# Mask, sums of exponentials and new memory in the tiling of the projections, and tile 0's projections in small pieces

## The chip, the cores and the metric

The kernel runs on one core of a Trainium2 chip. The metric is the device time of one execution in microseconds (us). The engines named below are TensorE (PE; its weight loads are listed apart as PEld), VectorE (DVE), ScalarE (ACT), GpSimd (POOL) and the queues that issue DMAs (SPq).

## What is computed

A block of text (2048 tokens of 512 numbers) goes through two branches, mixed by a gate for each token. Branch B is an MLP over all tokens at once. Branch A is attention with a recurrent memory: the tokens are cut into 64 segments of 32, and each segment's output for its eight memory rows is the next segment's memory, so the segments are one serial chain.

```python
def _A_ref(x, mem0, Wq, Wk, Wv, Wo, seg_len):      # H = 32 heads of 128, M = 8, seg_len = 32
    mask = (idx[:, None] < M) | (idx[:, None] >= idx[None, :])
    mem = mem0
    for s in range(n_seg):                          # 64 segments
        xs = x[:, s * seg_len:(s + 1) * seg_len, :].copy()
        h = jnp.concatenate([mem, xs], axis=1)      # 8 + 32 rows
        q = jnp.einsum('btd,dhe->bhte', h, Wq)      # k and v likewise
        ...
        scores = jnp.where(mask[None, None], scores, -1000000000.0)
        p = _softmax(scores, axis=-1)
        o = jnp.einsum('bhqk,bhke->bhqe', p, v)
        o = jnp.einsum('bhte,hed->btd', o, Wo)
        mem = o[:, :M, :].copy()                    # the next segment's memory
        outs.append(o[:, M:, :])

def _B_ref(x, w1, b1, w2, b2):
    y = _layernorm(x, axis=-1)
    h = _gelu(jnp.einsum('bsd,df->bsf', y, w1) + b1)
    return jnp.einsum('bsf,fd->bsd', h, w2) + b2

return g * a + (1 - g) * b                          # g = sigmoid((x * gate_w).sum(-1))
```

## The kernel before

The MLP comes first; then the loop over segments. Four segments make a tile of 128 tokens. A segment's first 24 tokens ride with its memory rows as 32 columns (`hT`); the last 8 tokens of each of the four segments are projected together ahead of time, as "side work" for the next tile (`left_v`, `left_qk`). Nearly all matmuls of the loop use a quarter of TensorE's array: 128 rows by 32 columns (`tile_position=(0, 32 * j)`), four side by side, written 128*32 in the profile. Attention over V uses 32 rows by 128 columns (32*128). The mask, the sums and the new memory use the whole array (128*128).

```python
def qk_unit(bk, G, t, h0, h1, kc):                                   # L211; v_unit is L222
    n = (h1 - h0) * 32
    for j in range(4):
        nc.tensor.matmul(bk[32 * j:32 * j + 32, 0:n], lhsT=G[:, kc, :], rhs=W5[t][:, kc, h0:h1, j, :],
                         start=(kc == 0), stop=(kc == KC - 1), tile_position=(0, 32 * j))

def left_qk(T, t, hf):                 # side work; left_v is built alike
    h0, h1 = HF[hf]
    bk = side([P, 512])
    side_k = side_n[0]
    for kc in range(KC):
        qk_unit(bk, GLs[T], t, h0, h1, kc)
        if kc < KC - 1:
            yield                      # a piece of four matmuls ends here
    def ev():
        ...                            # transpose and copies, queued for VectorE
    later(dve_q, ev, side_k)
    yield

def mask_mm():
    B = bank(7, [P, 512])
    S = B[:, 0:NG * EW].rearrange("p (i e) -> p i e", e=EW)
    nc.tensor.matmul(S, lhsT=ident[:], rhs=MkA[:].unsqueeze(2).to_broadcast([P, 4, 2, EW]),   # L360
                     start=True, stop=True, skip_group_check=True)
    return B, S
```

The projections of tile 0 have no segment to run beside, so they run beside the last three blocks of the MLP. Each `yield` of `setup` hands back to the MLP's loop over units (`up`: four matmuls, `down`: two).

```python
def setup():
    ...
    for vb in range(2):
        for _ in left_v(0, vb):        # all 16 matmuls at once
            pass
        flush(act_q)
        yield
    for hf in range(2):
        for t in range(2):
            for _ in left_qk(0, t, hf):
                pass
            flush(dve_q)
            yield
    left_v_in(0)
...
for u in range(NBLK * FC):             # 88 units of the MLP
    ...
    if blk >= NBLK - 3 and u % 4 == 0:
        next(pre, None)
```

A segment of the loop, cut:

```python
for bi, (t, h0, h1) in enumerate(BANKS):                     # projections of Q and K, L211
    ...
scores(S, s, 0, 3 * NG // 4)                                 # scores and V (L222) mixed
...
nc.scalar.activation(out=E[:, :, 0:16], in_=S[:, :, 0:16], func=ACTF.Exp, scale=scale, accum_out=hist[:, s, 0:1])     # L670
nc.scalar.activation(out=E[:, :, 16:EW], in_=S[:, :, 16:EW], func=ACTF.Exp, scale=scale, accum_out=hist[:, s, 1:2])
sm = bank(nc_, [P, NG, 8])
nc.tensor.matmul(sm[:], lhsT=BO[:], rhs=E[:, :, 8:16], start=True, stop=False)       # L673, first sums
nc.tensor.matmul(sm[:], lhsT=BO[:], rhs=E[:, :, 0:8], start=False, stop=True)        # L674
...
run_fill(5 + (si == 3))                                      # side work
nc.vector.reciprocal(out=R[:, 0:8 * NG]..., in_=sm[:])       # L677
nc.vector.tensor_tensor(out=Pm[:]..., ...)                   # L679
av(Um, 8, s, V, Pm, 8, 0, 0)                                 # attention of the memory rows, L384, L389
sr = B[:, 0:NG * 32].rearrange("p (i q) -> p i q", q=32)     # the mask's bank
nc.tensor.matmul(sr, lhsT=BO[:], rhs=E[:, :, 16:48], start=True, stop=False, skip_group_check=True)                   # L684, second sums
nc.tensor.matmul(sr[:, :, 24:32], lhsT=BO[:], rhs=E[:, :, 48:56], start=False, stop=True, skip_group_check=True)      # L685
...                                                          # Um to UTT, L688
nc.vector.reciprocal(out=R[:, 8 * NG:]..., in_=sr)           # L689
run_fill(1)                                                  # side work
for half in range(2):                                        # output projection, L233, and wsb, L708
    ...
S_next = mask_mm()                                           # the next segment's mask, L360
av_x(s - 1, (ne, na, nc_, nb))                               # attention of x of the segment before
run_fill(2 * (si == 3))                                      # side work, fourth segment of a tile only
for m in range(KC):                                          # new memory, L719
    nc.tensor.matmul(aT[:, m, :], lhsT=wsb[:, m * P:(m + 1) * P], rhs=Sel[:, 0:M], start=False, stop=True, skip_group_check=True)
nc.vector.tensor_copy(out=hn[:, :, 0:M], in_=aT)             # hT, L720
for _ in fill:                                               # the rest of the side work
    pass
```

Of the kernel before, what the change touches and what calls it, by code (L numbers as in the profile page):

```python
# [23 lines left out]
def kernel(ctx, tc, A_x, A_mem0, A_Wq, A_Wk, A_Wv, A_Wo, A_seg_len, B_x, B_w1, B_b1, B_w2, B_b2, gate_w, out):  # L24
    nc = tc.nc
    P = 128
    _, S, Dm = A_x.shape
    H, Dh = A_Wq.shape[1], A_Wq.shape[2]
    M = A_mem0.shape[1]
# [4 lines left out]
    KC = Dm // P  # L34
# [5 lines left out]
    EW = 16 + 40  # L40
# [212 lines left out]
    def left_qk(T, t, hf):  # L253
# [8 lines that stand above are left out]
            Tv = qk_tr(bk, h0, h1)  # L262
            if t == 0:
                nc.gpsimd.tensor_copy(out=QL[T % 2][:, h0:h1, :], in_=Tv)
            else:
                for hh in range(h0 // 8, h1 // 8):
                    r0 = 8 * hh - h0
                    nc.gpsimd.tensor_copy(out=KL[T % 2][:, :, :, hh, :], in_=Tv[:, r0:r0 + 8, :].rearrange("p g (s c) -> p g s c", c=LEFT))
        later(dve_q, ev, side_k)
        yield  # L270
# [81 lines left out]
    def prep_q(s):  # L352
        T, si = divmod(s, SPT)
        nc.gpsimd.tensor_copy(out=QT[:, :, 32:40], in_=QL[T % 2][:, :, LEFT * si:LEFT * si + LEFT])

    def mask_mm():

        B = bank(7, [P, 512])
        S = B[:, 0:NG * EW].rearrange("p (i e) -> p i e", e=EW)
        nc.tensor.matmul(S, lhsT=ident[:], rhs=MkA[:].unsqueeze(2).to_broadcast([P, 4, 2, EW]),  # L360
                         start=True, stop=True, skip_group_check=True)
        return B, S

    def scores(S, s, i0, i1):
# [119 lines left out]
    def setup():  # L484

        m0p = side([P, KC, M], BF16)
        for kc in range(KC):
            nc.tensor.transpose(m0p[:, kc, :], m0[:, kc * P:(kc + 1) * P], ident[:M, :M])
        nc.vector.tensor_copy(out=hT[0][:, :, 0:M], in_=m0p[:])
        x_left(0)  # L490
        x_left(1)
        prep_h(0)
        yield
        for vb in range(2):
            for _ in left_v(0, vb):
                pass
            flush(act_q)
            yield
        for hf in range(2):
            for t in range(2):  # L500
                for _ in left_qk(0, t, hf):
                    pass
                flush(dve_q)
                yield
        left_v_in(0)
# [21 lines left out]
    for u in range(NBLK * FC):  # L527
        blk, fc = divmod(u, FC)
        T1 = (blk + 1) * TB
        pend.append((u, up(u)))  # L530
        if fc == 2:
            c_act()
        if len(pend) > LAG:
            down(*pend.pop(0))
        if T1 < NT:
            if fc == 1 or fc == 3:
                ys[fc // 2] = norm(T1 + fc // 2)
            elif fc == 5 or fc == 7:
                norm_tr(T1 + fc // 2 - 2, ys[fc // 2 - 2])
        if blk % 2 == 0:  # L540
            if fc in (2, 5, 6, 7) and T1 + 2 < NT:
                bn(T1 + 2 + (2, 5, 6, 7).index(fc) )
            if fc == 8 and T1 + 2 < NT:
                newton(T1 + 2, T1 + 6)

        elif fc in (2, 4, 6, 8):
            T = T1 + (fc - 2) // 2
            if T < NT:
                gates(T, T + 1)
        elif fc == 10 and T1 < NT:  # L550
            gates2(T1, T1 + 4)
        if blk == 0 and fc in (9, 10):
            gates(fc - 9, fc - 8)
        if blk == 1 and fc == 0:
            gates2(0, 2)
        if blk == 1 and fc in (1, 3):
            gates(2 + fc // 2, 3 + fc // 2)
        if blk == 1 and fc == 9:
            gates2(2, 4)
        if blk == NBLK - 2 and fc == 8:  # L560
            ld_wo(H // 2, H)

        if blk >= NBLK - 3 and u % 4 == 0:
            next(pre, None)
    for a in pend:
        down(*a)
# [54 lines left out]
    for s in range(nseg + 2):  # L621
# [11 lines left out]
        if live:  # L633
            B, S = S_next
            na, nb, nc_, nd, ne = ring
            ring = (nd, ne, na, nc_, nb)
            qk_banks = (na, nb, nc_, nd, ne)
            if s >= 2:
                ux_out(s - 2)
                flush(act_q)  # L640
            if s + 1 < nseg:
                prep_h(s + 1)
            if s >= 1:
                prep_q(s)
                x_mul(s - 1)
            flush(dve_q)
            BANKS = [(0,) + HF[0], (1,) + HF[0], (0,) + HF[1], (1, H // 2, 3 * H // 4), (1, 3 * H // 4, H)]
            for bi, (t, h0, h1) in enumerate(BANKS):
                bk = bank(qk_banks[bi], [P, 512])
                for kc in range(KC):  # L650
                    qk_unit(bk, hc, t, h0, h1, kc)
                Tv = qk_tr(bk, h0, h1)
                dst = QT[:, h0:h1, 0:32] if t == 0 else KT[:, h0:h1, :]
                (nc.gpsimd.tensor_copy if bi == 2 else nc.scalar.copy)(out=dst, in_=Tv)  # L654
            V = cw.tile([P, NG, Dh], BF16, tag="V", name="V")
            Vs[s] = V
            vb0, vb1 = bank(na, [P, 512]), bank(nb, [P, 512])
            for kc in range(KC):
                v_unit(vb0, hc, 0, kc)
            nc.scalar.copy(out=v_out(V, 0), in_=vb0[:])  # L660
            flush(dve_q, 9)
            scores(S, s, 0, 3 * NG // 4)
            v_unit(vb1, hc, 1, 0)
            scores(S, s, 3 * NG // 4, NG)
            for kc in range(1, KC):
                v_unit(vb1, hc, 1, kc)
            E = cw.tile([P, NG, EW], BF16, tag="E", name="E")
            R = cw.tile([P, NG * 40], FP32, tag="R", name="R")
            Es[s], Rs[s] = E, R
            nc.scalar.activation(out=E[:, :, 0:16], in_=S[:, :, 0:16], func=ACTF.Exp, scale=scale, accum_out=hist[:, s, 0:1])  # L670
            nc.scalar.activation(out=E[:, :, 16:EW], in_=S[:, :, 16:EW], func=ACTF.Exp, scale=scale, accum_out=hist[:, s, 1:2])
            sm = bank(nc_, [P, NG, 8])
            nc.tensor.matmul(sm[:], lhsT=BO[:], rhs=E[:, :, 8:16], start=True, stop=False)  # L673
            nc.tensor.matmul(sm[:], lhsT=BO[:], rhs=E[:, :, 0:8], start=False, stop=True)  # L674
            nc.scalar.copy(out=v_out(V, 1), in_=vb1[:])
            run_fill(5 + (si == 3))
            nc.vector.reciprocal(out=R[:, 0:8 * NG].rearrange("p (i q) -> p i q", q=8), in_=sm[:])  # L677
            Pm = cw.tile([P, NG, 16], BF16, tag="Pm", bufs=1, name="Pm")
            nc.vector.tensor_tensor(out=Pm[:].rearrange("p i (a q) -> p i a q", q=8), in0=E[:, :, 0:16].rearrange("p i (a q) -> p i a q", q=8),  # L679
                                    in1=R[:, 0:8 * NG].rearrange("p (i q) -> p i q", q=8).unsqueeze(2).to_broadcast([P, NG, 2, 8]), op=ALU.mult)  # L680
            Um = [bank(k, [P, NG, 8]) for k in (nd, ne, na, nc_)]
            av(Um, 8, s, V, Pm, 8, 0, 0)
            sr = B[:, 0:NG * 32].rearrange("p (i q) -> p i q", q=32)
            nc.tensor.matmul(sr, lhsT=BO[:], rhs=E[:, :, 16:48], start=True, stop=False, skip_group_check=True)  # L684
            nc.tensor.matmul(sr[:, :, 24:32], lhsT=BO[:], rhs=E[:, :, 48:56], start=False, stop=True, skip_group_check=True)  # L685
            Tp, sp = divmod(s - 2, SPT)
            for j in range(4):
                (nc.scalar.copy if j % 2 else nc.vector.tensor_copy)(out=UTT[Tp % 2][:, :, j, 24 - 8 * sp:24 - 8 * sp + M], in_=Um[j][:])  # L688
            nc.vector.reciprocal(out=R[:, 8 * NG:].rearrange("p (i q) -> p i q", q=32), in_=sr)  # L689
            run_fill(1)  # L690
        else:
            if s == nseg:
                ux_out(s - 2)
                x_mul(s - 1)
                av_x(s - 1, (ne, na, nc_, 7))
            else:
                ux_out(s - 2)
            flush(dve_q)
            Tp, sp = divmod(s - 2, SPT)
# [15 lines left out]
        run_fill(2 * (si == 3))  # L715
        if s + 1 < nseg:
            aT = S_next[0][:, NG * EW:NG * EW + KC * M].rearrange("p (k m) -> p k m", m=M)
            for m in range(KC):
                nc.tensor.matmul(aT[:, m, :], lhsT=wsb[:, m * P:(m + 1) * P], rhs=Sel[:, 0:M], start=False, stop=True, skip_group_check=True)  # L719
            nc.vector.tensor_copy(out=hn[:, :, 0:M], in_=aT)  # L720
        for _ in fill:
            pass
# [142 lines left out]
```

## Time and profile before

| what | value |
|---|---|
| time, median of 3 runs | 834.87 us (834.65 to 835.76) |
| span of the profiled execution | 832.9 us |
| mean granted clock of TensorE | 0.998 |
| TensorE matmuls | 22405, busy 804.7 us |
| MLP's last three blocks with the projections of tile 0 | about 62 to 99.5 us of the span |
| loop over segments | from about 100 us on |
| an ordinary segment | 10.9 to 11.0 us, the fourth of a tile 11.7 us |

A line of the profile in order of time gives the start and the length in us, the engine, the line of the kernel, the operation, what is written and read, the shape, and how many instructions are merged; in brackets stands how long the engine was idle before, and whose work ended that. The shape 128*32 of a matmul is rows by columns of the array; 128x512 behind it is what streams through. Lengths of matmuls include their way through the array, so matmuls that follow one another closely overlap in the list; starts are the better measure. A share of busy time counts an engine as busy also while a matmul passes through.

### The profile page before, as it was taken

Reading aid. Unit: us, or ns where it says so; the run is one execution under the profiler, and the core shown is the slowest. Engines: PE = TensorE matmul, PEld = TensorE weight load, DVE = VectorE, ACT = ScalarE, POOL = GpSimd, SP = SyncE. Lnnn points to the kernel's source line nnn. Section 1 sums busy time; section 2 is a strip of 40 time slices with the busy share of each in tenths; the row PEclk is TensorE's granted clock in tenths of the full one; section 3 lists DMA queues with packets and bytes.
Section 4 is the critical chain, followed back from the end, with each engine's and each line's share of the span. In section 5 each row is a group of like instructions: output and inputs, shape, how many; then the busy total and the mean of one; then the engine's idle time right before and its main releaser. Section 6 shows DMA issues by size and latency. Waiting matters only on the chain.

```text
span 832.9 us, 49239 instructions
## 1 busy us (share of the span) xinstructions
PE 804.7 (97%) x22405; PEld 495.4 (59%) x22417; DVE 501.7 (60%) x1019; ACT 434.0 (52%) x1245; POOL 273.7 (33%) x625
## 2 busy tenths in 40 slices
PE   6999999999999999999999999999999999999886
PEld 4665555665666665566566556656656656665554
DVE  5764256565666566666656565656656665666553
ACT  3555544555455555555554555455555555555552
POOL 8000234242424333332424242434243243424220
PEclk9999999999999999999999999999999999999999
DMA  9791210100000010101010100000010101010000
GB/s 318 253 391 44 87 32 7 28 12 24 15 23 23 17 28 10 37 11 35 10 27 13 35 11 22 23 20 26 12 34 10 36 10 35 5 35 5 10 5 24
DMA packets 38216, 37.64 MB, mean 45 GB/s; under 512 B 13545, under 2 KB 36434, under 8 KB 36466
## 3 DMA queue, kind: packets, MB, share of 16 engines
q1 hardware_dynamic: 37874, 34.31, 12.4%
q8 instruction: 177, 2.90, 1.5%
q14 instruction: 37, 0.30, 0.1%
q0 software_dynamic: 128, 0.13, 0.1%
HBM read 26.03 MB, written 6.29 MB: 39 GB/s over the span
## 4 chain that ended last, share of the span: by engine, by line
PE 93%; DVE 3%; DMA 1%; issue 1%; SPq 1%; ACT 1%; DVEq 0%; ACTq 0%
PE b L211 35%; PE b L233 18%; PE b L222 17%; PE b L384 5%; PE hp L456 4%; PE bp L473 4%; PE b L360 2%; PE b L369 2%; PE b L684 2%; PE b L719 1%; PE b L389 1%; PE b L673 1%; DMA Wo_sb<-in_A_x_dram 1%; PE b L320 1%; PE b L373 0%
## 5 line engine op out<-in xcount | busy, mean ns | idle before, releaser
L217 DVE STREAM_TRANSPOSE Tt<-b 128x512 f32<-128x512 f32 (+1 forms) x384 | 225.6, 613 | 85.5 <-PE b L211 71.8
L211 PEld LDWEIGHTS <-hT 128*32 128x32 bf16 x5120 | 134.7, 97 | 100.0 <-DVE hT L720 15.4
L233 PE MATMUL b<-Wo_sb,UTT 128*32 128x256 bf16 (+1 forms) x4736 | 162.7, 285 | 1.2 <-ACT UTT L619 0.8
L222 PE MATMUL b<-Wv_sb,hT 128*32 128x512 bf16 x2048 | 141.9, 379 | 0.0
L211 PE MATMUL b<-Wq_sb,hT 128*32 128x512 bf16 x2048 | 132.9, 380 | 1.4 <-DVE hT L720 1.4
L211 PE MATMUL b<-Wk_sb,hT 128*32 128x256 bf16 (+1 forms) x3072 | 133.3, 308 | 0.0
L233 PEld LDWEIGHTS <-UTT 128*32 128x32 bf16 x4736 | 121.4, 97 | 19.1 <-ACT UTT L619 1.5
L654 ACT CAST KT<-Tt 128x256 bf16<-128x256 f32 (+1 forms) x192 | 87.1, 476 | 53.6 <-DVE Tt L217 53.6
L605 POOL TENSOR_TENSOR Px<-E,R 128x256 bf16<-128x256 bf16 x64 | 43.0, 672 | 218.7 <-DVE R L689 218.7
L689 DVE RECIPROCAL R<-b 128x256 f32<-128x256 f32 x64 | 112.5, 1757 | 0.0
L654 POOL CAST QT<-Tt 128x512 bf16<-128x512 f32 x64 | 39.1, 611 | 192.6 <-DVE Tt L217 192.6
L619 ACT CAST UTT<-b 128x256 bf16<-128x256 f32 x256 | 76.8, 387 | 23.9 <-PE b L389 23.4
L708 ACT CAST wsb<-b 128x256 bf16<-128x256 f32 x66 | 24.6, 372 | 120.1 <-PE b L233 120.1
L677 DVE RECIPROCAL R<-b 128x64 f32<-128x64 f32 x64 | 35.6, 557 | 79.4 <-PE b L674 79.4
L654 ACT CAST QT<-Tt 128x512 bf16<-128x512 f32 x64 | 39.6, 619 | 66.7 <-DVE Tt L217 66.7
L384 PEld LDWEIGHTS <-V 32*128 32x128 bf16 x4096 | 35.3, 91 | 46.2 <-DVE Pm L679 32.0
L222 PEld LDWEIGHTS <-hT 128*32 128x32 bf16 x2048 | 49.5, 96 | 21.1
L688 ACT CAST UTT<-b 128x64 bf16<-128x64 f32 x128 | 20.9, 215 | 75.2 <-PE b L389 75.2
L461 ACT ACTIVATE hg<-hp,b_sb 128x256 bf16<-128x256 f32 x80 | 37.7, 473 | 38.9 <-PE hp L456 38.9
L456 PE MATMUL hp<-yT,w_sb 128*128 128x256 bf16 (+1 forms) x352 | 53.8, 278 | 2.8 <-ACT hg L461 1.5
L607 POOL TENSOR_TENSOR racc<-racc,R 128x320 f32<-128x320 f32 x64 | 55.5, 867 | 0.0
L720 DVE CAST hT<-b 128x32 bf16<-128x32 f32 x63 | 12.1, 191 | 62.4 <-PE b L719 61.6
(116 smaller groups left out, 1075.2 us busy)
## 6 DMA issues: line engine op xcount, KB each, us to landing
Wv_sb<-in_A_Wv_dram SPq DMA_DIRECT2D x4, 1024.0 KB
Wq_sb<-in_A_Wq_dram SPq DMA_DIRECT2D x4, 1024.0 KB
Wk_sb<-in_A_Wk_dram SPq DMA_DIRECT2D x4, 1024.0 KB
Wo_sb<-in_A_Wo_dram SPq DMA_DIRECT2D x2, 2048.0 KB
vd<-vt SPq DMA_DIRECT2D x32, 128.0 KB
vs<-vd SPq DMA_DIRECT2D x256, 16.0 KB
out_dram<-o SPq DMA_DIRECT2D x16, 128.0 KB
Wo_sb<-in_A_x_dram SPq DMA_DIRECT2D x1, 1024.0 KB
```

What stands on the lines that cost most here:

```text
L211: nc.tensor.matmul(bk[32 * j:32 * j + 32, 0:n], lhsT=G[:, kc, :], rhs=W5[t][:, kc, h0:h1, j, :], start=(kc == 0), stop=(kc == KC - 1), til ...
L217: nc.vector.transpose(out=Tt[:, 0:n], in_=bk[:, 0:n])
L222: nc.tensor.matmul(bk[32 * j:32 * j + 32, :], lhsT=G[:, kc, :], rhs=Wv5[:, kc, 4 * vb:4 * vb + 4, j, :], start=(kc == 0), stop=(kc == KC - ...
L233: nc.tensor.matmul(bk[32 * g:32 * g + 32, :], lhsT=ut[:, i, j, c0:c0 + 32], rhs=Wo_sb[:, 4 * i + j, d0:d1], start=(j == 0 and i < 4), stop ...
L384: nc.tensor.matmul(U[j][:, i, :], lhsT=V[q, i, :], rhs=Pt[q, i, c_main:c_main + n], start=(i == 0), stop=False, skip_group_check=True, til ...
L456: nc.tensor.matmul(hp[:rows, :], lhsT=w1_sb[:, kc, fc * P:fc * P + rows], rhs=yTs[blk][:, kc, :], start=(kc == 0), stop=(kc == KC - 1))
L461: nc.scalar.activation(out=hg_[:rows, :], in_=hp[:rows, :], func=ACTF.Gelu_apprx_tanh, bias=b1_sb[:rows, fc:fc + 1], scale=1.0)
L605: nc.gpsimd.tensor_tensor(out=Px[:, :, 0:32], in0=E[:, :, 16:48], in1=Rr, op=ALU.mult)
L607: nc.gpsimd.tensor_tensor(out=racc[:], in0=racc[:], in1=R[:], op=ALU.add)
L619: nc.scalar.copy(out=UTT[T % 2][:, :, j, c0 + M:c0 + 40], in_=U[:])
L654: (nc.gpsimd.tensor_copy if bi == 2 else nc.scalar.copy)(out=dst, in_=Tv)
L689: nc.vector.reciprocal(out=R[:, 8 * NG:].rearrange("p (i q) -> p i q", q=32), in_=sr)
```

## The change

The mask, both sums of exponentials and the new memory are no longer one matmul over the whole array each, but four matmuls over 32 array columns each, side by side, which is the tiling of the projections. The purpose is that TensorE need not change its tiling there. On the other side, the projections of tile 0 beside the MLP's end no longer run as six whole blocks of 16 matmuls but in pieces of four, one piece after each MLP unit.

```diff
+    def sums(o, rhs, start, stop):
+        for j in range(4):
+            q = slice(32 * j, 32 * j + 32)
+            nc.tensor.matmul(o[q], lhsT=BO[:, q], rhs=rhs, start=start, stop=stop, skip_group_check=True, tile_position=(0, 32 * j))
+
+    def mem_out(aT, wsb):
+        for m in range(KC):
+            for c in range(4):
+                nc.tensor.matmul(aT[32 * c:32 * c + 32, m, :], lhsT=wsb[:, m * P + 32 * c:m * P + 32 * c + 32], rhs=Sel[:, 0:M],
+                                 start=False, stop=True, skip_group_check=True, tile_position=(0, 32 * c))
     def mask_mm():
-        nc.tensor.matmul(S, lhsT=ident[:], rhs=MkA[:].unsqueeze(2).to_broadcast([P, 4, 2, EW]),
-                         start=True, stop=True, skip_group_check=True)
+        for j in range(4):
+            q = slice(32 * j, 32 * j + 32)
+            nc.tensor.matmul(S[q], lhsT=ident[:, q], rhs=MkA[:].unsqueeze(2).to_broadcast([P, 4, 2, EW]),
+                             start=True, stop=True, skip_group_check=True, tile_position=(0, 32 * j))
...
         for vb in range(2):
-            for _ in left_v(0, vb):
-                pass
+            yield from left_v(0, vb)
             flush(act_q)
             yield
         for hf in range(2):
             for t in range(2):
-                for _ in left_qk(0, t, hf):
-                    pass
+                yield from left_qk(0, t, hf)
                 flush(dve_q)
                 yield
...
-        if blk >= NBLK - 3 and u % 4 == 0:
+        if blk >= NBLK - 3:
             next(pre, None)
...
-            nc.tensor.matmul(sm[:], lhsT=BO[:], rhs=E[:, :, 8:16], start=True, stop=False)
-            nc.tensor.matmul(sm[:], lhsT=BO[:], rhs=E[:, :, 0:8], start=False, stop=True)
+            sums(sm, E[:, :, 8:16], True, False)
+            sums(sm, E[:, :, 0:8], False, True)
...
-            nc.tensor.matmul(sr, lhsT=BO[:], rhs=E[:, :, 16:48], start=True, stop=False, skip_group_check=True)
-            nc.tensor.matmul(sr[:, :, 24:32], lhsT=BO[:], rhs=E[:, :, 48:56], start=False, stop=True, skip_group_check=True)
+            sums(sr, E[:, :, 16:48], True, False)
+            sums(sr[:, :, 24:32], E[:, :, 48:56], False, True)
...
-            for m in range(KC):
-                nc.tensor.matmul(aT[:, m, :], lhsT=wsb[:, m * P:(m + 1) * P], rhs=Sel[:, 0:M], start=False, stop=True, skip_group_check=True)
+            mem_out(aT, wsb)
```

## The prediction

> **What bounds the kernel now.** I read the busy shares first, then the chain that ended last, then one segment of the loop in order of time, and last the start times of all segments (the trace holds them to the nanosecond; the views round to 10 ns). Busy shares and chain:
>
> ```profile
> PE 804.7 (97%) x22405; PEld 495.4 (59%) x22417; DVE 501.7 (60%) x1019; ACT 434.0 (52%) x1245; POOL 273.7 (33%) x625
> PE 93%; DVE 3%; DMA 1%; issue 1%; SPq 1%; ACT 1%; DVEq 0%; ACTq 0%
> ```
>
> TensorE is the bound nearly everywhere. But busy is not useful: segment 5 in order of time (start, length, engine, line) shows where matmuls don't follow one another closely.
>
> ```profile
> 162.06 0.19 ACT L670 ACTIVATION_READ_ACCUMULATOR E<-b 128x1 f32 x1
> 162.35 0.20 PE L673 MATMUL b<-E,BO 128*128 128x64 bf16 x1
> 162.39 0.19 PE L674 MATMUL b<-E,BO 128*128 128x64 bf16 x1
> 162.51 1.05 PE L211 MATMUL b<-Wq_sb,GL 128*32 128x512 bf16 x16
> 162.62 0.56 DVE L677 RECIPROCAL R<-b 128x64 f32<-128x64 f32 x1 [1.64 <-PE b L674]
> 163.28 0.29 DVE L679 TENSOR_TENSOR Pm<-E,R 128x128 bf16<-128x128 bf16 x1
> 163.38 0.39 PE L211 MATMUL b<-Wk_sb,GL 128*32 128x512 bf16 x4
> 163.71 0.36 PE L384 MATMUL b<-Pm,V 32*128 32x8 bf16 x32
> ...
> 164.08 0.28 PE L684 MATMUL b<-E,BO 128*128 128x256 bf16 x1
> ...
> 164.20 0.19 PE L685 MATMUL b<-E,BO 128*128 128x64 bf16 x1
> ...
> 164.32 0.40 PE L211 MATMUL b<-Wk_sb,GL 128*32 128x512 bf16 x4
> 164.50 1.76 DVE L689 RECIPROCAL R<-b 128x256 f32<-128x256 f32 x1
> 164.55 1.92 PE L233 MATMUL b<-Wo_sb,UTT 128*32 128x256 bf16 x64
> ...
> 166.40 0.36 PE L360 MATMUL b<-MkA,ident 128*128 128x448 bf16 x1
> ...
> 167.09 0.26 PE L719 MATMUL b<-Sel,wsb 128*128 128x8 bf16 x4
> ...
> 167.27 0.61 PE L211 MATMUL b<-Wk_sb,GL 128*32 128x512 bf16 x8
> 167.38 0.19 DVE L720 CAST hT<-b 128x32 bf16<-128x32 f32 x1 [0.85 <-PE b L719]
> ...
> 167.71 0.61 PE L211 MATMUL b<-Wq_sb,hT 128*32 128x512 bf16 x8
> ```
>
> The 16 matmuls from 162.51 to 163.38 are four groups of four side by side: 0.87/4 = 0.217 us for 512 columns, about 2.4 columns per ns. With that rate I can say when a matmul has taken in its last column. The last L211 group starts at 163.38 and is through by 163.59; L384 starts at 163.71. L685 is through at 164.23; L211 starts at 164.32. Each time the tile shape changes (128*128, 128*32, 32*128), some 0.1 us is lost; where it stays 128*32 (164.32 to 164.55) the next starts within 4 ns. Over the loop I count 566 changes; the medians by kind lie between 93 and 109 ns, mostly 96 to 99. An ordinary segment has nine. So a change of shape costs **97 ns**, and this, not the matmuls' work, is what the new tiling can remove.
>
> **What the Trainium skill says.** "TensorEngine Tiling (Array Packing)", Key Properties: "Changing tiling mode (not just tile) drains the TensorE". The trace agrees and supplies the size, 97 ns. "TensorE: Matmul & The Clock Gate", The mechanism: matmuls on different tiles overlap, about 4 ns from start to start; here four of a group start 3 to 5 ns apart. So four matmuls of 448 columns on 32 array columns each should take the 187 ns of the one they replace. "TensorEngine Tiling", Instruction Overhead: a matmul of few columns costs about 60 cycles whatever its size; here, groups of four with 8 columns each follow one another every 25 ns (L384), and the score matmuls, in the projections' tiling, every 26. "GPSIMD Engine Reference", 1. Specifications: GpSimd shares its SBUF interfaces with VectorE, in contention with two-input VectorE instructions. The trace fits that in the third segment of each four: the product Pm takes 403 ns instead of 292 while GpSimd copies VL.
>
> **The change, part by part.**
> *Work.* Mask: 1 matmul becomes 4, 187 ns either way. The sums: 4 become 16, in two groups each, same columns. New memory (L719): 4 become 16, four groups x 26 = 104 ns, against about 115 now. So 27 more matmuls a segment, no more time.
>
> *Changes of shape.* Now: V to sums, sums to side projections, those to attention (32*128), attention to the second sums, sums to side projections, output projection to mask, mask to attention of x, that to new memory, new memory to projections: nine. After: only around the two attentions: four. Five go, and six in the fourth segment of each tile, which has side work before the new memory too. 5.25 x 97 x 64 = 32.6 us if TensorE waited for nothing else. But each change hides another engine's latency, so I measure what ends next at each:
>
> a) V to first sums. Now 99 ns after V's last column. E's accumulator read ends 91 ns before the sums start, and the shortest such distance in the loop, a real wait, is 51. Gain 91 - 51 = **40**.
>
> b) Sums to attention. Now 1358 ns from start to start. The side work without its first change would take 1262. The other path (reciprocal, Pm, semaphore) shows itself where there is no side work, in segment 3:
>
> ```profile
> 140.61 0.20 PE L673 MATMUL b<-E,BO 128*128 128x64 bf16 x1
> ...
> 141.89 0.36 PE L384 MATMUL b<-Pm,V 32*128 32x8 bf16 x32 [1.05 <-DVE Pm L679]
> ```
>
> 141.89 - 140.61 = 1.28 us. Gain 1358 - 1281 = **77**. In the third segment Pm is late (1393 now, ending 58 ns after Pm): gain **0**. In the fourth, with 24 side matmuls (1574 now): the full **96**.
>
> c) Second sums to mask, 2321 ns now. Two changes go (193 ns), but the mask writes the bank that the long reciprocal (L689, 1.76 us) reads. The reciprocal ends 146 ns before the mask; a wait on VectorE ends 55 ns after its cause (hT to projections, where they do wait). Gain 146 - 55 = **91**, the rest becomes waiting.
>
> d) Mask to attention: that change is 109 ns from 128*128 and 98 from 128*32: **11**.
>
> e) New memory to next projections, 628 ns now. Through hT: 90 + 206 + 192 + 55 = 543; through the side work without the change: 535. Gain about **80**. In the fourth segment it is already bound by hT (539): gain 0, perhaps -8 for the later last matmul, but the change ahead of the new memory gives **98**.
>
> Sums: first and second segment 40+77+91+11+80 = 299; third 222; fourth 40+96+91+11+98-8 = 328. Segments 4 to 59 are 14 of each: 14 x (299+299+222+328) = 16.1 us. Segments 0 to 2 and 63 give about 0.2 to 0.3 each; 3 and 60 to 62, without side work, about 0.09 each: 1.4 together. **Loop: -17.5 us.**
>
> *Projections of tile 0 in the MLP.* Now six blocks of 16:
>
> ```profile
> 72.01 0.59 PE L473 MATMUL bp<-w_sb,hg 128*128 128x512 bf16 x2
> 72.54 1.05 PE L222 MATMUL b<-Wv_sb,GL 128*32 128x512 bf16 x16
> 73.52 0.64 PE L456 MATMUL hp<-yT,w_sb 128*96 128x256 bf16 x4
> ```
>
> Each has a change before and after it (95 to 99 ns in all six). After, the built order shows 24 pieces of four matmuls, each between two MLP units: 48 changes instead of 12. TensorE is busy 37.08 of 37.5 us there and GELU (0.47 us of the 0.87 us unit) isn't the bound, so nothing hides them: 36 x 97 = **+3.5 us**.
>
> **Sum:** 834.9 - 17.5 + 3.5 = 820.9, say 821.
>
> **Rivals.**
> 1. *All removed drains are time:* 32.6 - 3.5 = 29 us, 806. For it: TensorE carries 93% of the chain. Against: the distances in a, b, c and e are measured and smaller than a drain.
> 2. *Waits eat nearly everything:* VectorE's chain from sums to mask binds already in one segment of four; if the finer sums ended later (16 matmuls with loads of 32 columns instead of 128) or hT came later, b, c and e would each lose 30 to 50 ns more. Then the loop gains about 9 us: 829. Against: side by side matmuls are this kernel's normal form and keep their pace.
> 3. *The MLP pieces cost nothing or less* (pieces falling into waits): 817.5. Against: that stretch has no waits to fall into.
> 4. *27 matmuls and 27 weight loads more a segment* bind the issue: 27 x 25 ns would be 0.7 us a segment, +43 us. Against: score matmuls pass one every 6.5 ns, loads included.
>
> **Range and chances.** The loop's gain may be off by 3 us (rivals 1 and 2 in part), the MLP's loss by 1. 818.2 to 824.5 holds 8 in 10. Faster by over 2% means below 818.2, which needs 20 us from the loop, or the MLP for nothing: 0.11. Slower by over 2% needs rival 4: 0.01. Within 2%: 0.88.
>
> **What would show it.** In the trace after: no gap at V to sums beyond about 59 ns, none between sums and side projections, and between output projection and mask a wait on the reciprocal of about 60 ns. Attention waiting on Pm and projections waiting on hT should appear in the list of waits, some 50 times each, by tens of ns. A segment should be 0.30, 0.30, 0.22 and 0.33 us shorter by its place in the tile; the MLP stretch some 3.5 us longer, with 48 changes. The prediction is wrong if four matmuls side by side take longer than the one, if waits on VectorE are longer than 55 ns from their cause, or if a change costs less between the MLP's pieces.

## The result, and the profile after

| | before | after |
|---|---|---|
| time, median | 835.08 us (4 runs, 834.65 to 835.76) | 839.53 us (4 runs, 837.85 to 840.54) |
| span of the profiled execution | 832.9 us | 836.1 us |
| start of the first mask (end of the MLP) | 100.12 us | 105.02 us |
| loop, from the first mask on | 732.8 us | 731.1 us |
| instruction DMA packets of queue q8 | 177 | 190 |

The ratio of the times is 1.0051, with a 95% interval of 1.0032 to 1.007: the kernel became slower by half a per cent, where I had predicted 821. The granted clock is the same (0.996 against 0.998).

The busy shares and the chain that ended last, of the kernel after:

```profile
PE 801.4 (96%) x24120; PEld 503.6 (60%) x24133; DVE 503.9 (60%) x1019; ACT 434.4 (52%) x1245; POOL 273.8 (33%) x625
PE 91%; DVE 4%; issue 2%; DMA 1%; SPq 1%; ACT 1%; DVEq 0%; ACTq 0%
```

TensorE is busy 3.3 us less, as the change meant it, and carries two points less of the chain. One went to VectorE, one to "issue", which is time in which TensorE stood still and waited for nothing that the profile shows. Both are what this document is about.

Segment 9 of the kernel after in order of time (start, length, engine, line); it stands at the same place in its tile as segment 5, which the prediction shows of before:

```profile
211.30 0.19 ACT L681 ACTIVATION_READ_ACCUMULATOR E<-b 128x1 f32 x1
211.55 0.24 PE L360 MATMUL b<-E,BO 128*32 128x64 bf16 x8
211.60 1.05 PE L211 MATMUL b<-Wq_sb,GL 128*32 128x512 bf16 x16
211.84 0.56 DVE L688 RECIPROCAL R<-b 128x64 f32<-128x64 f32 x1 [1.62 <-PE b L360]
212.50 0.29 DVE L690 TENSOR_TENSOR Pm<-E,R 128x128 bf16<-128x128 bf16 x1
212.85 0.36 PE L398 MATMUL b<-Pm,V 32*128 32x8 bf16 x32
...
213.22 0.32 PE L360 MATMUL b<-E,BO 128*32 128x256 bf16 x8
213.37 0.39 PE L211 MATMUL b<-Wk_sb,GL 128*32 128x512 bf16 x4
...
213.67 1.76 DVE L700 RECIPROCAL R<-b 128x256 f32<-128x256 f32 x1
...
215.48 0.37 PE L374 MATMUL b<-MkA,ident 128*32 128x448 bf16 x4
...
216.17 0.27 PE L365 MATMUL b<-Sel,wsb 128*32 128x8 bf16 x16
...
216.57 0.19 DVE L730 CAST hT<-b 128x32 bf16<-128x32 f32 x1 [0.86 <-PE b L365]
...
216.82 1.05 PE L211 MATMUL b<-Wq_sb,hT 128*32 128x512 bf16 x16
```

The gaps at the changes of shape are gone as planned: sums to side work is 0.05 us, and the mask starts 54 ns after the reciprocal L700 ends (213.67 + 1.76 = 215.43). But look at the last three lines. From the start of the new memory to the copy hT there are 0.40 us; before, there were 0.30 (167.09 to 167.38). The sixteen matmuls start within 99 ns, the four of before within 90, and yet VectorE starts 0.1 us later.

The places of the prediction, measured over segments 4 to 59 from start times in the trace (medians in ns; "4th" is the fourth segment of a tile, "3rd" the third):

| step | from, to | before | predicted | after |
|---|---|---|---|---|
| a | V's last column to the first sums | 99 | 59 | 60 |
| b | first sums to attention, 1st and 2nd | 1357 | 1280 | 1305 |
| b | the same, 3rd and 4th | 1393, 1573 | 1393, 1477 | 1434, 1470 |
| c | second sums to mask | 2321 | 2230 | 2258 |
| d | mask to attention of x | 295 | 284 | 305 |
| e | new memory to projections, 1st to 3rd | 628 | 548 | 646 |
| e | the same, 4th; last attention matmul to new memory, 4th | 540; 656 | 548; 558 | 605; 550 |

The waits of TensorE in the kernel after (engine and line, for what: us in total, times, longest):

```profile
PE b L398 <- DVE Pm L690: 5.3, 5, 1.1
...
PE b L211 <- DVE hT L730: 1.9, 5, 0.4
PE b L398 <- issue: 1.6, 5, 0.5
PE b L403 <- issue: 1.6, 4, 0.5
PE b L365 <- issue: 1.0, 4, 0.4
```

Before, the whole list has two such "issue" lines of 0.3 us or less at a time. The new ones are pauses of half a microsecond in the middle of rows of equal matmuls. One of them, TensorE and VectorE in order of time:

```profile
182.49 0.26 PE L365 MATMUL b<-Sel,wsb 128*32 128x8 bf16 x15
...
183.13 0.17 PE L365 MATMUL b<-Sel,wsb 128*32 128x8 bf16 x1 [0.38 <-issue]
...
183.33 0.19 DVE L730 CAST hT<-b 128x32 bf16<-128x32 f32 x1 [1.31 <-PE b L365]
```

Fifteen of the sixteen matmuls of the new memory have run, and the sixteenth comes half a microsecond later, though it needs nothing that they did not need.

To keep the two apart I use two measures from here on. **Undisturbed loop**: for each place in the tile, the lower quartile of the segments' periods, summed over the 56 segments 4 to 59. **Pauses**: what the 56 periods have above that. Before: 625.0 and 3.0 us. After: 618.2 and 8.6 us. Pauses are of one execution each, for both kernels the fastest of the four; up to 1 us more or less depends on where a segment is taken to begin. So the profiled execution after is 3.2 us longer for these reasons: the stretch up to the first mask +4.9; the undisturbed loop -6.8; pauses +5.6; the rest of the loop -0.5. Of the 4.9, the trace puts 3.95 on the 24 pieces and 0.95 on the start, where the MLP waits longer for its first weights (1.9 us against 0.7), which has nothing to do with the change.

Two pieces in the MLP of the kernel after, by start times:

```profile
72.84 0.40 PE L222 MATMUL b<-Wv_sb,GL 128*32 128x512 bf16 x4
73.17 0.61 PE L470 MATMUL hp<-yT,w_sb 128*128 128x256 bf16 x4
73.62 0.59 PE L487 MATMUL bp<-w_sb,hg 128*128 128x512 bf16 x2
...
74.15 0.40 PE L222 MATMUL b<-Wv_sb,GL 128*32 128x512 bf16 x4
```

Four matmuls of 512 columns stream for about 0.22 us, and L470 follows 0.33 after the start of the piece: a full change of shape, which the trace has at 109 ns on this side and 96 on the other.

### The profile page after: what moved, and what is told of

It is laid out like the page before. It is cut to its first block, busy times and chain, and to the rows that moved or that the text cites. A ratio compares the mean times of both kernels' runs of the same rounds, so it can differ in the third digit from the quotient of the medians.

```text
span 836.1 us, 52672 instructions
## 1 busy us (share of the span) xinstructions
PE 801.4 (96%) x24120; PEld 503.6 (60%) x24133; DVE 503.9 (60%) x1019; ACT 434.4 (52%) x1245; POOL 273.8 (33%) x625
## 4 chain that ended last, share of the span: by engine, by line
PE 91%; DVE 4%; issue 2%; DMA 1%; SPq 1%; ACT 1%; DVEq 0%; ACTq 0%
PE b L211 32%; PE b L233 18%; PE b L222 16%; PE b L398 5%; PE hp L470 4%; PE bp L487 4%; PE b L360 3%; PE b L374 2%; PE b L383 2%; PE b L365 2%; PE b L403 1%; DVE R L688 1%; DMA Wo_sb<-in_A_x_dram 1%; DVE Pm L690 1%; PE b L387 0%
## 5 line engine op out<-in xcount | busy, mean ns | idle before, releaser
L211 PEld LDWEIGHTS <-hT 128*32 128x32 bf16 x5120 | 135.1, 97 | 108.1 <-DVE hT L730 25.7
L211 PE MATMUL b<-Wq_sb,hT 128*32 128x512 bf16 x2048 | 135.3, 380 | 3.4 <-DVE hT L730 1.9
L211 PE MATMUL b<-Wk_sb,hT 128*32 128x256 bf16 (+1 forms) x3072 | 136.0, 308 | 0.0
L233 PEld LDWEIGHTS <-UTT 128*32 128x32 bf16 x4736 | 119.7, 97 | 23.7 <-DVE UTT L699 12.4
L700 DVE RECIPROCAL R<-b 128x256 f32<-128x256 f32 x64 | 112.5, 1757 | 0.0
L222 PEld LDWEIGHTS <-hT 128*32 128x32 bf16 x2048 | 51.2, 96 | 20.7
L470 PE MATMUL hp<-yT,w_sb 128*128 128x256 bf16 (+1 forms) x352 | 54.9, 281 | 3.2 <-DMA w_sb<-in_B_w_dram 1.9
```

The source lines that it names most:

```text
L222: nc.tensor.matmul(bk[32 * j:32 * j + 32, :], lhsT=G[:, kc, :], rhs=Wv5[:, kc, 4 * vb:4 * vb + 4, j, :], start=(kc == 0), stop=(kc == KC - ...
L233: nc.tensor.matmul(bk[32 * g:32 * g + 32, :], lhsT=ut[:, i, j, c0:c0 + 32], rhs=Wo_sb[:, 4 * i + j, d0:d1], start=(j == 0 and i < 4), stop ...
L470: nc.tensor.matmul(hp[:rows, :], lhsT=w1_sb[:, kc, fc * P:fc * P + rows], rhs=yTs[blk][:, kc, :], start=(kc == 0), stop=(kc == KC - 1))
```

## The experiments

All ratios are to the kernel before, run beside it on the same chip, with their 95% intervals. A letter in an expectation is the name of a theory; F is the one that TensorE pauses because its program is fetched in pieces.

**The change taken apart.** Only the pieces in the MLP, the loop as before:

```diff
-            for _ in left_v(0, vb):
-                pass
+            yield from left_v(0, vb)
...
-        if blk >= NBLK - 3 and u % 4 == 0:
+        if blk >= NBLK - 3:
```

> The kernel before with only the pieces of four matmuls after each MLP unit; nothing in the loop changes. Theory A: 48 changes of tiling instead of 12 at 96 ns in and 109 ns out, and 11 ns for the first MLP matmul after: +3.9 us, 839. Rival B: no difference, 835. The stretch from the transposes of the memory to the first mask gets 3.9 us longer, and the loop stays within 1 us.

Measured: 838.31 us against 835.47, ratio 1.0033 (1.0021 to 1.0045): +2.8 us. In its trace the pieces take the 3.95 us again. The undisturbed loop is 625.0, as before; its pauses are 1.9 us, 1.1 less than in the trace of before, and 3.95 - 1.1 is about the 2.8 measured.

The reverse, the changed loop with tile 0's projections in whole blocks:

```diff
-            yield from left_v(0, vb)
+            for _ in left_v(0, vb):
+                pass
```

> The changed kernel, but tile 0's projections run as six whole blocks again; the loop is as changed. Theory A (three causes: pieces in the MLP cost about 4 us by their 36 further drains; the loop's gain of 7 us in undisturbed segments is eaten by pauses of TensorE without a wait, and by signals of the tiled matmuls that come later): about 4 us less than the changed kernel, 835 to 836, ratio to before 0.998 to 1.003. Rival B (the pieces are harmless and the loop itself is slower): stays at 839. Rival C (the loop did gain the predicted 17 us and something outside it lost more): below 825.

Measured: 837.28 us (22 runs from 834.15 to 840.77), ratio 1.0026 (1.0015 to 1.0036), 1 to 2 us more than expected. The changed loop alone is thus no gain but a small loss. Its undisturbed part is 618.1, but the pauses are 11.8 us. The same loop has 8.6 us of them in the kernel after, but these are two single executions, and the times of this kernel alone spread over 6.6 us: that the code ahead of the loop makes the difference is not shown.

The loop's three parts alone, each in the kernel before; first the mask:

```diff
-        nc.tensor.matmul(S, lhsT=ident[:], rhs=MkA..., ...)
+        for j in range(4):
+            q = slice(32 * j, 32 * j + 32)
+            nc.tensor.matmul(S[q], lhsT=ident[:, q], rhs=MkA..., ..., tile_position=(0, 32 * j))
```

> The kernel before with only the mask as four tiled matmuls (three more a segment, none where hT is waited for). One change of tiling less, but the mask then waits for the long reciprocal: from the reciprocal's end to the mask 54 ns instead of 146, and mask to attention 10 ns longer: 82 ns a segment, 5.2 us: 830 to 831.5. If all of a drain became time: 6.2 us, 829.6. If later signals of tiled matmuls or pauses eat it: 834 or more.

The sums of exponentials alone (four matmuls become sixteen, in the `sums` helper of the change):

> The kernel before with only both sums tiled. First sums: 40 ns from the wait on E, then 52, -41 and 103 ns on the way to attention by place in the tile; second sums: about 41 ns until the mask (its own change of tiling stays): undisturbed segments gain 133, 133, 40 and 184 ns, 6.9 us; pauses a little more frequent: 829 to 833. Rival (later signals eat the drains): 835.

The new memory alone (four become sixteen, in `mem_out`):

> The kernel before with only the new memory as sixteen tiled matmuls. The change of tiling after it goes, but hT's signal comes some 100 ns later: new memory to projections 646 instead of 628 ns in three segments of four, and 33 ns gained in the fourth: about 0 in undisturbed segments. 24 more instructions where the program is densest: pauses grow from 3 us to some 8: 838 to 842. Rival (the prediction's step e: gain of 80 ns a segment): 830.

And mask and sums together, the new memory whole:

> The kernel before with mask and sums in the tiling of the projections; the new memory stays four matmuls over the whole array, tile 0's projections stay whole blocks. Theory A: hT's signal is back at 206 ns and no instructions are added where the program is densest but 15 matmuls a segment elsewhere; undisturbed segments gain 144, 144, 51 and 195 ns by their place in the tile, 8 us with the ends, pauses a little more frequent (3 to 6 us instead of 3): 827 to 830. Rival (the tiled sums cost as much by their later signals as their drains bring): 835.

| kernel | time, us | ratio (95%) | undisturbed loop | pauses |
|---|---|---|---|---|
| before, as first profiled | 835.08 | | 625.0 | 3.0 |
| mask alone | 833.33 | 0.9962 (0.9949 to 0.9974) | 620.3 | 5.6 |
| sums alone | 831.38 | 0.9943 (0.9926 to 0.9960) | 618.0 | 4.4 |
| new memory alone | 838.33 | 1.0024 (1.0017 to 1.0031) | 625.5 | 5.2 |
| mask and sums | 832.41 | 0.9962 (0.9950 to 0.9974) | 617.6 | 8.3 |
| changed loop, whole blocks | 837.28 | 1.0026 (1.0015 to 1.0036) | 618.1 | 11.8 |

Three things follow. The new memory is the part that spoils the loop: it brings nothing undisturbed and adds pauses. The mask and the sums gain 4.7 and 7.0 us undisturbed when alone, but 7.4 together, because one reciprocal limits both: with the mask tiled alone, the mask comes 2229 ns after the second sums, with both tiled 2259, since the reciprocal then starts later. And the pauses grow with every part that is tiled. They are also why the mask alone and mask and sums took 2 us longer than I had expected.

**Why hT comes late.** First, whether sixteen matmuls in place of four are the reason. This kernel leaves the new memory whole, and adds twelve matmuls that add zeros:

```diff
-            for m in range(KC):
-                nc.tensor.matmul(aT[:, m, :], ..., rhs=Sel[:, 0:M], ...)
+            for rep in range(4):
+                for m in range(KC):
+                    nc.tensor.matmul(aT[:, m, :], ..., rhs=Sel[:, 0:M] if rep == 0 else SelX[:, RIDE:32], ...)
```

> The kernel before, but the new memory takes sixteen matmuls over the whole array instead of four: twelve more that add zeros. Their last signal to the copy of hT: if it comes late because of the number of small matmuls in a row, about 300 ns after the last one's start; if it comes late because of the tiling to 32 columns, the 206 ns of before. In either case a segment gets about 0.3 us longer (12 x 25 ns on the path to the next segment), about +19 us in all, and more if pauses of TensorE become more frequent with 24 more instructions a segment.

Measured: from the last matmul to hT 204 ns, against 206 with four whole ones and 300 with sixteen tiled ones. So it isn't their number as such. (Time 857.03, one run: sixteen whole ones take longer themselves.)

Then the changed loop with only some of the sixteen tiled matmuls; hT takes their rows for all four blocks of 128, so most of the new memory is left out and the time is only an indication:

```diff
-        for m in range(KC):
-            for c in range(4):
+        for m in range(1):
+            for c in range(n):          # n = 4, 2, 1
                 nc.tensor.matmul(aT[32 * c:32 * c + 32, m, :], ...)
```

Four:

> The changed loop with whole blocks in the MLP, but the new memory leaves out three of its four parts: four tiled matmuls instead of sixteen, and the copy of hT spreads the one part over all four. If the late signal (300 ns) comes from sixteen small matmuls or their weight loads piling up, it falls to 200 to 240 ns and a segment gets 0.1 us shorter, 829 or so; if it comes from the tiling itself, it stays near 300 and only some 75 ns of starts go where hT is waited for.

Two:

> As with one tiled matmul, but with the first two, side by side; the copy takes their 64 rows. If each group of columns adds its part: 225 to 245 ns from the last matmul to the copy to hT, about half way between one and four. If it is the tiling itself: 270 to 300, as with four. Time 822 to 827 us.

One:

> The changed loop with tile 0's projections in whole blocks, and of the new memory's 16 tiled matmuls only the first: the copy to hT takes its 32 rows for all four, so most of the new memory is left out. Measured so far, from the last matmul of the new memory to the copy to hT: whole array 204 to 206 ns (with 4 or with 16 matmuls), 16 tiled 300 ns after the attention (270 after side work), 4 tiled 290 (249). If it is the four groups of columns side by side that are late (each adds its part): one tiled matmul alone gives 200 to 220 ns. If it is the tiling itself, or the change of tiling just before: 270 to 300 also with one. The time is that of the four tiled matmuls or less, 822 to 827 us.

Measured from the last matmul to hT, in the first three segments of a tile and in the fourth: four tiled 290 and 249 ns (826.01 us, ratio 0.9881, 0.9863 to 0.9898), two 278 and 238 (827.29 us, one run), one 273 and 233 (824.03 us, one run). A single tiled matmul is already late. That is the number I had expected if the tiling itself, or the change of tiling just before, were the reason; "200 to 220", for groups of columns that each add their part, did not come. Yet there is a small rise from one to sixteen, and the fourth segments are 30 to 40 ns earlier with the same tiling, so tiling alone doesn't explain it either. The kernel before, and the one with a single tiled matmul, new memory and hT in order of time:

```profile
211.52 0.26 PE L719 MATMUL b<-Sel,wsb 128*128 128x8 bf16 x4
211.82 0.19 DVE L720 CAST hT<-b 128x32 bf16<-128x32 f32 x1 [0.85 <-PE b L719]
```

```profile
210.84 0.18 PE L365 MATMUL b<-Sel,wsb 128*32 128x8 bf16 x1
211.12 0.18 DVE L734 CAST hT<-b 32x32 bf16<-32x32 f32 x1 [0.99 <-PE b L365]
```

One matmul and 0.27 to 0.28 us; four matmuls and 0.30 us from the first of them. The answer is in the trace's semaphore updates. TensorE's semaphore is raised by the last matmul into each of the four banks of the attention of x, and then by the last matmul of the new memory. VectorE starts 23 or 24 ns after that last update in all of these kernels, so the update itself is late. Medians, first segment of a tile:

| new memory | from one attention update to the next | from the last of them to the new memory's | last matmul to its update |
|---|---|---|---|
| 1 tiled | 34 ns | 34 ns | 250 ns |
| 2 tiled | 34 | 42 | 255 |
| 4 tiled | 34 | 59 | 267 |
| 16 tiled (after) | 34 | 159 | 278 |
| 4 whole (before) | 34 | 59 | 183 |
| 16 whole | 34 | 355 | 180 |

The third column of the tiled rows is 34 + 8.3 (n - 1): 34, 42, 59, 159. These numbers are those of a queue: completions of matmuls leave TensorE one after another, 8.3 ns each, and 34 where one raises a semaphore. Small tiled matmuls start faster than that (40 of the attention start within 0.27 us, 7.0 ns each, the last four with an update; sixteen of the new memory within 99 ns, 6.6 each), so the queue grows, and the new memory's update is its end. Already the last update of the attention comes 326 ns after its matmul. With four whole ones the queue is just through (183 ns, where 180 is what it takes in a fourth segment, with nothing before it); sixteen whole ones start 26 ns apart and never queue. It fits the pause shown above too: when the sixteenth matmul came alone, hT started 0.20 us after it. In the fourth segments, where four side matmuls and not the attention stand ahead, the update comes 210, 218, 236 and 336 ns after the first of 1, 2, 4 and 16 tiled matmuls: again 8.4 for each further one. That a single tiled one takes 210 there and not 180 fits four completions of the side matmuls ahead of it (4 x 8.3 = 33), but no run separates these from a cost of the tiling itself.

The same fits the sums. Four matmuls side by side end together, and the last of their completions passes 3 x 8.3 = 25 ns after the first: first sums to the update 246 ns before and 271 after (38 + 208, 49 + 222), second sums 327 and 355 (120 + 207, 130 + 225).

The Trainium skill has part of this, in "TensorE: Matmul & The Clock Gate", The cost: per-tile semaphore tail, on the page I cited: increments serialize, and the tail grows by 26.3 ns for each increment and 4.7 for each tile. The trace has 34 - 8.3 = 26 for an increment, as the page says, and 8.3 for a tile, not 4.7.

**Where the pauses come from.** They lie at one place of the program. The instruction packets of q8 are 16 KB, and the Trainium skill, "Perfetto Trace Analysis", The 4-stage abstract model, gives an instruction 64 bytes: 256 instructions. The trace agrees: 177 packets for 44822 matmuls and weight loads before (175 x 256 = 44800), 190 for 48253 after. Packets start some 4 us apart and take 0.9 to 1.4 us. Theory F: where a stretch runs faster than the program comes, TensorE waits for it.

I counted each matmul with its weight load as two instructions from the program's start (with the 12 or 13 matmuls put back that some traces lack), and took those matmuls of segments 4 to 59 that start over 150 ns later than is usual at their place. In every kernel but those with 512 columns below, all but five at most of them are number 184 modulo 256 (182 in the two kernels with pieces): 6 of 10 before, 20 of 23 after, 31 of 35 in the changed loop with whole blocks. Most of the others stand in nearly every kernel at the same work (three scores, one of the sums; 1.2 us together). One packet comes for each 256 instructions, so each such place has its own, the last that landed before it in nearly all cases. Where TensorE pauses, the matmul starts 1.2 to 1.6 us after that packet has landed (1.19 to 1.57 after, 1.24 to 1.45 before, 1.23 to 1.61 with whole blocks). Where it doesn't, the packet has landed up to some 4 us before; but in none of these kernels does a matmul at this place start within 1.19 us of its packet's landing. The pause on the sixteenth matmul above is one of them: its packet had landed 1.35 us before.

To take instructions away, the output projection writes 512 columns with one matmul instead of two of 256: 32 matmuls and 32 loads a segment fewer, for the same columns.

```diff
-        for half in range(2):
-            d = slice(256 * half, 256 * half + 256)
-            wp = bank((nb, nd)[half], [P, 256])
-            for u in range(8):
-                wo_unit(wp, UTT[Tp % 2], 24 - 8 * sp, u, 256 * half, 256 * half + 256)
+        wp = bank(nd, [P, Dm])
+        for u in range(8):
+            wo_unit(wp, UTT[Tp % 2], 24 - 8 * sp, u)
```

In the kernel before:

> The kernel before with only the output projection in matmuls of 512 columns. Theory F: pauses without a wait (3.0 us over segments 4 to 59) shrink to under 1 us, 832 to 833. Rival: 835 or above.

In the kernel with mask and sums tiled:

> As the run before (mask and sums tiled), and the output projection runs 512 columns a matmul in one bank instead of twice 256: 32 matmuls and 32 weight loads a segment fewer for the same columns, 1.75 us. Theory F (pauses of TensorE come from fetching its program in pieces of 256 instructions): the 256 densest instructions now take over 3.5 us instead of about 3, the pauses nearly vanish: 3 to 5 us less than without, 823 to 826. Rival (pauses have another cause, semaphores or memory): no change, or slower, since the first half of wsb now is copied after the last matmul.

In the changed loop with whole blocks:

> The changed loop (mask, sums and new memory tiled) with whole blocks in the MLP, and the output projection in matmuls of 512 columns. Theory F: the changed loop's pauses (some 12 us over segments 4 to 59 in its profile with whole blocks) shrink to 1 or 2 us; the undisturbed segments stay as they are: 837 less 8 to 11, that is 826 to 829. Rival (pauses belong to the tiled matmuls as such): 836 to 838.

| kernel | time, us | ratio (95%) | undisturbed loop | pauses, without and with this edit |
|---|---|---|---|---|
| before, 512 columns | 845.83 | 1.0119 (1.0104 to 1.0134) | 635.4 | 3.0, 0.9 |
| mask and sums, 512 columns | 843.30 | 1.0093 (1.0078 to 1.0108) | 628.5 | 8.3, 0.9 |
| changed loop, 512 columns | 839.50 | 1.0051 (1.0038 to 1.0064) | 626.0 | 11.8, 1.5 |

The pauses go in all three: not one is left at the place above, where matmuls now start at the earliest 1.97, 1.68 and 1.30 us after their packet. But the times are 10 us and more above those that I had expected, for a reason of its own: the two halves of wsb now lie in one bank, and ACT's copy waits for VectorE's. (Of mask and sums, the profiled execution took 839.93 us at a granted clock of 0.999; the other three, at 0.990 to 0.994, took 843.1 to 843.9.) The kernel before with 512 columns, in order of time:

```profile
168.90 0.42 DVE L706 CAST wsb<-b 128x256 bf16<-128x256 f32 x1 [0.24 <-PE b L233]
169.36 0.37 ACT L707 CAST wsb<-b 128x256 bf16<-128x256 f32 x1 [2.39 <-DVE wsb L706]
169.46 0.53 PE L718 MATMUL b<-Sel,wsb 128*128 128x8 bf16 x4
```

The new memory stretches to 0.53 us, where it takes 0.26 in the kernel before: its second half waits for the second copy. In three segments of four that is 0.25 us each, 10.6 us in all, which is what the undisturbed loop of the kernel before lost (10.4).

As slower segments by themselves might calm the pauses, I turned it round: the kernel before, with the side matmuls of 512 columns split into two of 256 each. That adds 24 matmuls and 24 loads a segment and removes no change of shape.

```diff
-            qk_unit(bk, GLs[T], t, h0, h1, kc)
+            for d in range(2):          # from tile 1 on; left_v alike
+                for j in range(4):
+                    nc.tensor.matmul(bk[32 * j:32 * j + 32, 256 * d:256 * d + 256], lhsT=GLs[T][:, kc, :],
+                                     rhs=W5[t][:, kc, h0 + 8 * d:h0 + 8 * d + 8, j, :], ...)
```

> The kernel before, but each side matmul of 512 columns (from tile 1 on) is split into two of 256: 24 more matmuls and loads a segment with the same columns in the same tiling, and no change of shape removed. Theory F (TensorE fetches its program in pieces and pauses where 256 instructions pass too fast): the pauses without a wait rise from 3 us to 6 to 12 us although nothing else is faster, and the undisturbed segments stay within 4 us in sum of before (625). Time 838 to 844. Rival (the pauses come with the removed changes of shape, whatever the number of instructions): pauses stay at 3 us, time 835 to 838.

Its busy shares show that TensorE has nearly the matmuls of the kernel after:

```profile
PE 808.6 (96%) x23857; PEld 532.0 (63%) x23857; DVE 501.7 (60%) x1019; ACT 434.2 (52%) x1245; POOL 273.8 (33%) x625
```

Measured: 841.08 us against 836.23, ratio 1.0063 (1.0040 to 1.0087). The pauses are 6.0 us against 3.0, at the lower edge of what F expected, and outside the rival's; the undisturbed loop is 627.1, 2.0 more (sums to attention +13 ns). At the place above there are 14 pauses of 5.1 us together, against 6 of 1.9 before. So the number of instructions alone brings pauses. That TensorE waits there for its program rests on the one place in 256 and on the steady lag behind the packet; the wait itself has no record, and what the 1.2 us after the landing are is open.

**The part of the change that pays.** Mask and first sums tiled; second sums and new memory whole; projections of tile 0 in whole blocks:

```diff
-            sums(sr, E[:, :, 16:48], True, False)
-            sums(sr[:, :, 24:32], E[:, :, 48:56], False, True)
+            nc.tensor.matmul(sr, lhsT=BO[:], rhs=E[:, :, 16:48], start=True, stop=False, skip_group_check=True)
+            nc.tensor.matmul(sr[:, :, 24:32], lhsT=BO[:], rhs=E[:, :, 48:56], start=False, stop=True, skip_group_check=True)
```

> The kernel before with mask and first sums tiled; second sums and new memory whole. The second sums' signal is then not late, so the reciprocal and with it the mask come 29 ns earlier than with all sums tiled, and the drain that stays lies in the shade of the reciprocal; 12 instructions a segment fewer. Undisturbed segments gain 174, 174, 81 and 225 ns, 9.5 us; with pauses of 3 to 6 us: 826 to 829, faster than mask and both sums (832.4). If pauses depend only on where the pieces of program fall, anything from 826 to 832.

Measured: 829.76 us (828.57 to 830.57), ratio 0.9919 (0.9902 to 0.9936), which beats both kernels. Second sums, reciprocal and mask of a segment, in order of time:

```profile
208.04 0.28 PE L691 MATMUL b<-E,BO 128*128 128x256 bf16 x1
...
208.46 1.76 DVE L696 RECIPROCAL R<-b 128x256 f32<-128x256 f32 x1
...
210.27 0.37 PE L367 MATMUL b<-MkA,ident 128*32 128x448 bf16 x4
```

Whole second sums let the reciprocal start 0.42 us after them, tiled ones 0.45 (213.22 to 213.67 above). The side matmuls behind them pay a change of shape in return, but they have the time: the reciprocal decides when the mask may start, 2230 ns after the second sums, the number of step c. Undisturbed loop 615.9 (-9.1), pauses 6.6.

## Why the prediction was wrong

The change of shape, 97 ns, was the right thing to look at, and the ends of the removed ones came as worked out wherever no signal of the new matmuls was waited for. Step by step:

- **a, V to first sums, gain 40:** right, 39.
- **b, sums to attention, 77 and 96:** 52 in the first two segments, -41 in the third, 103 in the fourth. "The sums: ... in two groups each, same columns" was right for TensorE and wrong for its signal: the reciprocal starts 25 ns later after the sums' first matmul. In the third segment Pm itself also took longer (421 ns against 404) beside GpSimd's copy of VL. Where side work carries the path, in the fourth, the gain is there.
- **c, sums to mask, 91:** 63. The reciprocal starts 29 ns later; the wait of 55 ns behind it is as predicted, 54.
- **d, mask to attention, 11:** -10. The change from 128\*32 costs no less here, and the last of the four mask matmuls starts 10 ns after the first.
- **e, new memory to projections, 80:** -18, and -65 in the fourth segment instead of -8; the change ahead of it gave 106, predicted 98. This is the step that failed most: "90 + 206 + 192 + 55" took the signal of the four whole matmuls, 206, for that of sixteen tiled ones, which is 300 (270 in the fourth). The sum is 99 + 300 + 192 + 55 = 646.

Over the 56 segments the shortfall is 14 x (3 x 98 + 57 - 8) = 4.8 us for e, 1.6 for c, 14 x (25 + 25 + 41 - 7) = 1.2 for b and 1.2 for d: 8.8 of the 9.3 us by which the undisturbed gain (6.8) missed the 16.1. The whole miss in the profiled executions, from -14.0 to +3.2, is these 9.3, the 5.6 of pauses, 0.45 of the pieces, 0.95 of the start, and 0.9 of the gain outside segments 4 to 59 (0.5 instead of 1.4).

- **"So 27 more matmuls a segment, no more time":** wrong apart from all this. They cost 5.6 us of pauses in the profiled execution. Rival 4 asked for the issue of each instruction, found it fast enough, rightly, and so missed that the program has to arrive as well.
- **The pieces, +3.5:** right in kind and about in size: 3.95 by the trace, +2.8 in the run with them alone.

Of the rivals, the second had the mechanism ("if the finer sums ended later ... or hT came later") but 30 to 50 ns for e, where it was 98, and for b and c, where it was 25 to 41; its 829 holds the pieces but no pauses, without whose 5.6 us the profiled execution would have taken 832. The first and the third fell. Of the signs that I named, the gaps at the sums and the wait of the mask are there. Waits on Pm and hT "some 50 times each" are not in the list of waits (5 each): it counts an engine as busy while a matmul still passes through, so waits of tens of ns show only in start times.

## What to carry to other kernels

Before small matmuls are cut into tiles to save a change of shape, ask who waits for them. Where only TensorE follows, the gain is the whole change (103 and 106 ns in the fourth segments); where another engine waits for the result, the update comes after all completions in front of it, and cutting finer lengthens that queue. Where a loop is near its limit in instructions, count those as well: a cut that adds instructions without columns can lose by pauses what it gains in work, so cut only the parts that pay (here mask and first sums, 0.9919), and leave the others whole.

## What I had not expected of the hardware

- Completions of small matmuls pass one at a time: 8.3 ns each, 34 ns where one raises a semaphore. After 40 small matmuls with four updates, even a single further one is heard of only 250 ns after its start (210 after side work); a small whole one with nothing queued takes 180.
- TensorE pauses for 0.2 to 0.8 us at one place in each 256 instructions, never starting there earlier than 1.19 us after the 16 KB packet of program has landed. The pauses grow when instructions are added (14 instead of 6 for 24 matmuls and 24 loads more a segment) and are gone with 32 of each fewer.
